# The middle phase of a long convolution, regrouped by pairs of frequencies

## The chip, the core and the metric

The kernel runs on one core of a Trainium2 chip. A core has a tensor engine (PE, which multiplies matrices into PSUM; its weight loads are listed as PEld), a vector engine (DVE), a scalar engine (ACT), GpSimd (POOL) and a sync engine (SP), which here only issues transfers. The engines run side by side and wait for each other by semaphores. DVE and ACT read PSUM, POOL does not. Transfers between HBM and SBUF are issued from SP's and ACT's queues and run on 16 DMA engines. The metric is the time of one execution on the device in microseconds (us); less is better.

## The reference

The input has 4 batches of 12800 positions with 128 channels. A small network with a decaying window makes a filter of the length of the sequence, one per channel. The product of `x` and `v` is convolved with it causally, by real Fourier transforms of twice the length; the result times `x` then passes a gated block.

```python
h_filt = (np.maximum(pos_emb @ w1, 0.0) @ w2) * window
u = x * v
Uf = np.fft.rfft(u, n=2 * S, axis=1)
Hf = np.fft.rfft(h_filt, n=2 * S, axis=0)
y = np.fft.irfft(Uf * Hf[None], n=2 * S, axis=1)[:, :S]
a = x * y
gate = sigmoid(sum(conv_w[k] * shifted(a, k) for k in range(5)))
out = (gate * (a @ w_val)) @ w_out
```

## The kernel before

The sequence is cut into two blocks (J = 2) of M = 6400 = N1 x N2 = 100 x 64 samples. Each block is evaluated at 6400 complex points, k = k1 + 100 k2, in two stages: a transform over 100 samples that yields k1, then one over 64 that yields k2. With U0, U1 the spectra of the two signal blocks and H0, H1' those of the filter (H1' is H1 - i H0), the inverse is applied to H0 U0 for the first block and to H0 U1 + H1' U0 for the second.

The kernel has three phases, one after the other.

Phase 1 makes the filter and the first stage of all spectra and stores the latter to HBM (`a_u`). Two of its matmuls, L200 and L201, give 64 columns each and write the two halves of PSUM's partitions. Phase 3 runs the inverse's second stage and the gated block. The change leaves both alone.

Phase 2 is a loop over the 100 values of k1. A step holds 128 partitions, the 64 real parts and the 64 imaginary parts of k2. It loads `a_u` (L351, two k1 a transfer) and the second stage's matrices (`wt`, eight k1 a transfer) from SP's queue. PE makes the filter's spectrum (`h_ps`, L360), which ACT copies to SBUF in four pieces (L364) so that one tile holds the real parts on both halves, the other the imaginary parts. PE makes the spectra of the two blocks (`z_ps`, L367), 4 batches x 128 channels each. A complex product needs real and imaginary part in the same partition; so ACT makes a copy `zsw` of `z_ps` with the halves exchanged and one of them negated (L299, L300). DVE multiplies `z_ps` by the filter's real parts (L311 for H0 U0 and H0 U1, L312 for H1' U0, into `v_t`), and POOL multiplies `zsw` by the imaginary parts (the same two lines, into `q_t`).

A step later DVE adds `q_t` to `v_t` (L316) and the second block's two terms (L317, 448 of 512 columns; POOL adds the other 64 two steps later, L320). Three steps later PE applies the inverse's first stage (`c_ps`, L326), ACT copies the result (L327) and issues its store to `c_y` (L328).

No planner reorders this: in the trace each engine runs phase 2's instructions in the order in which the loop writes them, and the framework puts the semaphores.

Of the kernel before, what the change touches and what calls it, by code (L numbers as in the profile page):

```python
# [9 lines left out]
F32 = mybir.dt.float32  # L10
F32R = mybir.dt.float32r
I32 = mybir.dt.int32
AF = mybir.ActivationFunctionType
ALU = mybir.AluOpType
# [3 lines left out]
# The causal convolution of length S = 2 * M is cut in two blocks of M = N1 * N2 samples,  # L18
# n = n1 * N2 + n2. A block's polynomial is evaluated at the M roots of z^M = i,
# k = k1 + N1 * k2, in two stages (over n1, then over n2 with the twiddles in the matrix).  # L20
# With z^M = i a product of two real blocks comes back as (low half) + i (high half), so
#   y0 = Re inv(H0 U0),   y1 = Re inv(H0 U1 + (H1 - i H0) U0)
# and no block is padded.
B, S, D, FO, KC = 4, 12800, 128, 64, 5
J, N1, N2 = 2, 100, 64
M = N1 * N2
KG = 8
# [6 lines left out]
def _tables():  # L34
# [10 lines left out]
    w = np.transpose(np.concatenate([f, g], 2), (1, 0, 2))  # L45
# [11 lines left out]
def _narrow(nc, pool, dst, src):  # L57
    """dst (float32) = src, whose 64-bit words are doubles, rounded to nearest."""
    p, n = dst.shape
# [12 lines left out]
    # the 29 bits below, in units of the value's own power of two  # L72
# [6 lines left out]
    # below float32's range: zero  # L79
# [7 lines left out]
def tile_longconv_gate(  # L87
# [24 lines left out]
    # spectra after the first stage: [k1][re|im][n2][block][...][d]  # L112
    a_u = dram.tile([N1, 2, N2, J, B, D], F32, name="a_u")
    # products after the inverse's first stage: [block][batch][k1][re|im, n2][d]
# [27 lines left out]
    def load():  # L142
        return ld.tile([128, 2048], F32, name="ld")
# [10 lines left out]
    # the filter's channels before w2, after the first stage: [re|im, n2][k1][block][channel]  # L154
# [4 lines left out]
    with tc.tile_pool(name="p1", bufs=1) as p1, tc.tile_pool(name="ps1", bufs=1, space=PSUM) as ps1:  # L159
# [4 lines left out]
        def filt():  # L164
# [25 lines left out]
            # block 1 holds H1 - i H0  # L190
# [14 lines left out]
            # the second stage, in place: [block, channel][k1][re|im, k2]  # L205
# [70 lines left out]
        # the filter's steps are spread over the signal's by their time on the tensor engine  # L276
# [16 lines left out]
    with tc.tile_pool(name="p2", bufs=1) as p2, tc.tile_pool(name="ps2", bufs=1, space=PSUM) as ps2:  # L293
        BD = B * D
        CUT = 64

        def tail(k1, g_l, z_ps, h_sb):
            zsw = p2.tile([128, J, BD], F32, name="zsw", bufs=2)
            nc.scalar.activation(zsw[0:N2], z_ps[N2:2 * N2], AF.Copy, scale=-1.0)  # L299
            nc.scalar.copy(out=zsw[N2:2 * N2], in_=z_ps[0:N2])  # L300

            def h_b(c, j, rep):
                a = h_sb[:, c, j]
                return a.unsqueeze(1).to_broadcast([128, rep, D])

            # [V0 | H0 U1 | H1' U0], then the last two added
            v_t = p2.tile([128, J + 1, BD], F32, name="v_t2", bufs=4)
            q_t = p2.tile([128, J + 1, BD], F32, name="q_t", bufs=3)
            fl = lambda t: t.rearrange("p j (b d) -> p (j b) d", d=D)
            for t, z, eng, c in ((q_t, zsw, nc.gpsimd, 1), (v_t, z_ps, nc.vector, 0)):  # L310
                eng.tensor_tensor(fl(t[:, 0:J]), fl(z), h_b(c, 0, J * B), op=ALU.mult)  # L311
                eng.tensor_tensor(fl(t[:, J:J + 1]), fl(z[:, 0:1]), h_b(c, 1, B), op=ALU.mult)  # L312
            return v_t, q_t

        def sums(v_t, q_t):
            nc.vector.tensor_tensor(v_t, v_t, q_t, op=ALU.add)  # L316
            nc.vector.tensor_tensor(v_t[:, 1, CUT:], v_t[:, 1, CUT:], v_t[:, 2, CUT:], op=ALU.add)  # L317

        def sums_rest(v_t, q_t):
            nc.gpsimd.tensor_tensor(v_t[:, 1, :CUT], v_t[:, 1, :CUT], v_t[:, 2, :CUT], op=ALU.add)  # L320

        def inverse(k1, g_l, v_t):
            c_sb = p2.tile([128, J, B, D], F32, name="c_sb", bufs=3)
            for j in range(J):
                c_ps = ps2.tile([128, BD], F32, name="c_ps", bufs=2)
                nc.tensor.matmul(out=c_ps, lhsT=g_l, rhs=v_t[:, j], start=True, stop=True)  # L326
                nc.scalar.copy(out=c_sb[:, j].rearrange("p b d -> p (b d)"), in_=c_ps)  # L327
            nc.scalar.dma_start(  # L328
                out=c_y[:, :, k1].rearrange("j b p d -> p (j b) d"),
                in_=c_sb.rearrange("p j b d -> p (j b) d"))  # L330

        SKEW = 3
        ready = []

        def advance(k1):
            for lag, do in ((1, sums), (2, sums_rest)):
                if 0 <= k1 - lag < N1:
                    do(*ready[k1 - lag][2:])
            if k1 >= SKEW:
                inverse(*ready[k1 - SKEW][:3])  # L340

        for k1 in range(N1):
            if k1 % KG == 0:
                n_k = min(KG, N1 - k1)
                wt = load().rearrange("p (k e) -> p k e", k=KG)
                nc.sync.dma_start(out=wt[:, 0:n_k], in_=t_w[:, k1:k1 + n_k])
            if k1 % 2 == 0:
                a2 = load().rearrange("p (k j e) -> p k j e", k=2, j=J)
                step = 1 if k1 == 0 else 2
                for i in range(0, 2, step):  # L350
                    nc.sync.dma_start(  # L351
                        out=a2[:, i:i + step].rearrange("p k j e -> p k (j e)"),
                        in_=a_u[k1 + i:k1 + i + step].rearrange("k c n j b d -> (c n) k (j b d)"))
            au = a2[:, k1 % 2]
            wk = wt[:, k1 % KG]
            f_l = wk[:, 0:2 * N2]
            g_l = wk[:, 2 * N2:4 * N2]

            h_ps = ps2.tile([128, J, D], F32, name="h_ps", bufs=2)
            nc.tensor.matmul(out=h_ps, lhsT=ag[:, k1].rearrange("p j e -> p (j e)"), rhs=w2bd, start=True, stop=True)  # L360
            h_sb = p2.tile([128, 2, J, D], F32, name="h_sb2", bufs=3)
            for c in range(2):
                for half in range(2):
                    nc.scalar.copy(out=h_sb[half * N2:(half + 1) * N2, c], in_=h_ps[c * N2:(c + 1) * N2])  # L364
            z_ps = ps2.tile([128, J, BD], F32, name="z_ps", bufs=2)
            for j in range(J):
                nc.tensor.matmul(out=z_ps[:, j], lhsT=f_l, rhs=au[:, j], start=True, stop=True)  # L367
            ready.append((k1, g_l) + tail(k1, g_l, z_ps, h_sb))
            advance(k1)
        for k1 in range(N1, N1 + SKEW):  # L370
            advance(k1)
# [5 lines left out]
    with tc.tile_pool(name="p3", bufs=1) as p3, tc.tile_pool(name="ps3", bufs=1, space=PSUM) as ps3:  # L377
# [5 lines left out]
        def conv_out(b, j, ext, rows=None):  # L383
            """y of one block, times x, transposed: ext[d, HALO + token]; with rows, a list
# [244 lines left out]
```

## Time and profile before

| what | value |
|---|---|
| median of 3 runs | 1739.79 us (1730.27 to 1749.66) |
| profiled execution, span of its instructions | 1744.1 us |
| mean granted clock of PE | 0.887 |
| busy in the span | PE 77%, DVE 81%, ACT 59%, POOL 67% |
| phase 2, first product of k1 = 0 to that of k1 = 98 | 478.1 to 1080.6 us |
| first load of `c_y` for phase 3 | issued at 1102.7 us |

A group's row gives line, engine, operation, output <- inputs, shapes and count, then the busy time in us and the mean of one in ns, then the idle time of the engine ahead of it and what ended most of it. A row of the timeline gives start and length in us, then the same names, and at the end the number of instructions merged into it. Busy time counts an instruction from its start, so time in which a started instruction is held up by another engine is counted as busy.

### The profile page before, as it was taken

How to read it: one execution, taken by the hardware profiler on the slowest of the kernel's cores; microseconds unless marked ns; L12 is line 12 of the kernel's file. 1: busy time of each engine (PE TensorE's matmuls, PEld its weight loads, DVE VectorE, ACT ScalarE, POOL GpSimd, SP SyncE). 2: the span in 40 equal slices, each digit the busy share in tenths (PEclk: the TensorE clock that was granted, in tenths of full speed). 3: DMA queues.
4: the chain of work that ended last, by engine and by line, in shares of the span. 5: the costliest groups of instructions: out<-in, count | busy, mean ns of one | idle time of the engine just before them, and what ended most of it. 6: DMA issues, size and time to landing. Idle time of an engine off the chain costs nothing.

```text
span 1744.1 us, 16766 instructions
## 1 busy us (share of the span) xinstructions
PE 1344.8 (77%) x5313; PEld 873.4 (50%) x5313; DVE 1418.7 (81%) x1204; ACT 1032.3 (59%) x1657; POOL 1168.2 (67%) x528
## 2 busy tenths in 40 slices
PE   4679988767677777677777676588888888889896
PEld 3567766544323333233333232356766676667675
DVE  5663337653399999999999999269999999999996
ACT  2235446552477777677777775255656565556765
POOL 2223333333299988878888888159978697788752
PEclk9798997885799989998999999687988998888899
DMA  6666666666656656555656553565555455555512
GB/s 227 243 243 241 246 236 234 241 235 253 220 203 198 212 181 205 179 177 181 203 178 211 173 185 99 170 216 168 183 191 158 159 183 161 172 177 166 177 61 91
DMA packets 224831, 332.97 MB, mean 191 GB/s; under 512 B 7832, under 2 KB 162500, under 8 KB 220108
## 3 DMA queue, kind: packets, MB, share of 16 engines
q1 hardware_dynamic: 99358, 226.12, 38.8%
q10 hardware_dynamic: 125386, 105.79, 18.3%
q8 instruction: 43, 0.70, 0.2%
q14 instruction: 44, 0.36, 0.1%
HBM read 200.80 MB, written 131.07 MB: 190 GB/s over the span
## 4 chain that ended last, share of the span: by engine, by line
DVE 43%; DMA 21%; issue 15%; PE 15%; ACT 3%; POOL 2%; SPq 1%; ACTq 0%; POOLq 0%; DVEq 0%
DVE gt L462 16%; DMA a_u<-st 13%; DVE v_t L316 9%; DVE v_t L317 5%; PE fp L264 4%; DMA ld<-c_y 4%; DVE v_t L311 3%; DVE v_t L312 3%; DMA ld<-in_x_dram 3%; DVE at L413 2%; PE o_ps L506 2%; DVE gd L495 2%; PE y_ps L412 2%; PE z_ps L367 1%; PE c_ps L326 1%
## 5 line engine op out<-in xcount | busy, mean ns | idle before, releaser
L447 POOL TENSOR_TENSOR lo<-ld,hi 100x1024 fp32r<-100x1024 f32 x117 | 373.0, 3209 | 116.9 <-ACT hi L444 115.2
L462 DVE SCALAR_TENSOR_TENSOR gt<-ext,cw,gt 128x1280 f32<-128x1280 f32 (+1 forms) x164 | 411.5, 2521 | 10.2 <-POOL gt L459 5.3
L238 POOL TENSOR_TENSOR u_lo<-u_t,u_hi 100x1024 fp32r<-100x1024 f32 x64 | 154.2, 2411 | 302.3 <-ACT u_hi L237 263.5
L367 PE MATMUL z_ps<-ld 128*128 128x512 f32 x400 | 215.7, 666 | 117.3 <-DVE v_t L312 97.7
L311 POOL TENSOR_TENSOR q_t<-zsw,h_sb 128x1024 f32<-128x1024 f32 x100 | 241.6, 2416 | 90.2 <-ACT zsw L300 90.2
L316 DVE TENSOR_TENSOR v_t<-v_t,q_t 128x1536 f32<-128x1536 f32 x100 | 277.6, 2806 | 1.2 <-POOL q_t L312 1.2
L326 PE MATMUL c_ps<-v_t,ld 128*128 128x512 f32 x400 | 208.0, 639 | 57.2 <-POOL v_t L320 29.1
L312 POOL TENSOR_TENSOR q_t<-zsw,h_sb 128x512 f32<-128x512 f32 x100 | 225.8, 2258 | 0.0
L364 ACT COPY h_sb<-h_ps 64x256 f32<-64x256 f32 x400 | 147.1, 368 | 103.0 <-DVE v_t L312 66.7
L264 PE MATMUL fp<-u_hi,fwd_hi 100*100 100x512 f32 x256 | 127.6, 499 | 90.3 <-ACT st L267 59.3
L269 DVE COPY st<-fp 100x512 f32<-100x512 f32 x128 | 84.6, 687 | 127.9 <-DMA a_u<-st 100.0
L367 PEld LDWEIGHTS z_ps<-ld 128*128 128x128 f32 x400 | 76.6, 206 | 205.8 <-issue 166.9
L506 PEld LDWEIGHTS o_ps<-wout,gd 128*128 128x128 f32 x700 | 167.9, 320 | 11.9 <-issue 2.5
L317 DVE TENSOR_TENSOR v_t<-v_t 128x448 f32<-128x448 f32 x100 | 172.6, 1757 | 0.1
L444 ACT CAST hi<-ld 100x1024 fp32r<-100x1024 f32 x128 | 128.0, 1048 | 71.1 <-DMA ld<-c_y 44.5
L326 PEld LDWEIGHTS c_ps<-v_t,ld 128*128 128x128 f32 x400 | 77.9, 205 | 179.2 <-issue 123.3
L506 PE MATMUL o_ps<-wout,gd 128*128 128x128 f32 x700 | 164.2, 384 | 0.7 <-DVE gd L495 0.7
L299 ACT ACTIVATE zsw<-z_ps 64x1024 f32<-64x1024 f32 x100 | 102.2, 1022 | 61.1 <-PE z_ps L367 56.9
L311 DVE TENSOR_TENSOR v_t<-z_ps,h_sb 128x1024 f32<-128x1024 f32 x100 | 121.1, 1211 | 18.5 <-ACT zsw L300 18.5
L267 ACT COPY st<-fp 100x512 f32<-100x512 f32 x128 | 69.7, 591 | 110.7 <-DMA a_u<-st 85.6
L237 ACT CAST u_hi<-u_t 100x1024 fp32r<-100x1024 f32 x64 | 68.0, 1064 | 107.1 <-PE fp L264 51.6
L236 DVE TENSOR_TENSOR u_t<-ld 100x1024 f32<-100x1024 f32 x64 | 82.5, 1290 | 57.0 <-POOL u_lo L238 49.9
(93 smaller groups left out, 2696.8 us busy)
## 6 DMA issues: line engine op xcount, KB each, us to landing
c_y<-c_sb ACTq DMA_DIRECT2D x100, 512.0 KB
ld<-c_y SPq DMA_DIRECT2D x64, 800.0 KB
ld<-a_u SPq DMA_DIRECT2D x49, 1024.0 KB
ld<-in_x_dram SPq DMA_DIRECT2D x66, 400.0 KB
ld<-in_v_dram SPq DMA_DIRECT2D x64, 400.0 KB
a_u<-st ACTq DMA_DIRECT2D x64, 400.0 KB
a_u<-st SPq DMA_DIRECT2D x64, 400.0 KB
ld<-in_x_dram SPq DMA_DIRECT2D x31, 800.0 KB
```

What stands on the lines that cost most here:

```text
L238: nc.gpsimd.tensor_tensor(lo, u_t, hi.bitcast(F32), op=ALU.subtract)
L264: nc.tensor.matmul(out=fp, lhsT=w[:, c], rhs=d[:, b:b + 2], start=(k == 0), stop=(k == 2))
L311: eng.tensor_tensor(fl(t[:, 0:J]), fl(z), h_b(c, 0, J * B), op=ALU.mult)
L312: eng.tensor_tensor(fl(t[:, J:J + 1]), fl(z[:, 0:1]), h_b(c, 1, B), op=ALU.mult)
L316: nc.vector.tensor_tensor(v_t, v_t, q_t, op=ALU.add)
L317: nc.vector.tensor_tensor(v_t[:, 1, CUT:], v_t[:, 1, CUT:], v_t[:, 2, CUT:], op=ALU.add)
L326: nc.tensor.matmul(out=c_ps, lhsT=g_l, rhs=v_t[:, j], start=True, stop=True)
L364: nc.scalar.copy(out=h_sb[half * N2:(half + 1) * N2, c], in_=h_ps[c * N2:(c + 1) * N2])
L367: nc.tensor.matmul(out=z_ps[:, j], lhsT=f_l, rhs=au[:, j], start=True, stop=True)
L447: eng.tensor_tensor(lo[:, :, hs], ct[:, :, hs], hi[:, :, hs].bitcast(F32), op=ALU.subtract)
L462: nc.vector.scalar_tensor_tensor(gt, sl(k), cw[:, k:k + 1], gt, op0=ALU.mult, op1=ALU.add)
L506: nc.tensor.matmul(out=o_ps[:, i], lhsT=gv[:, g0 + i], rhs=wout, start=True, stop=True)
```

## The change

Only phase 2 and the order of the table `w` change. The loop now goes over 50 pairs of k1. The two k1 of a pair lie on the two halves of the partitions, 64 k2 each, and real and imaginary parts lie in separate tiles. So a spectrum tile is made by two matmuls of 64 columns, one for each half, and an inverse tile by matmuls of 64 rows that add the real and the imaginary contribution in PSUM. ACT no longer exchanges halves; it copies the filter's spectrum as (real, imaginary) and as (-imaginary, real). All products are made by DVE from PSUM, the four of block 0 in two instructions 2048 wide, the two of block 1 in two 1024 wide. POOL only adds the two parts of the products, 2048 and 1024 wide. DVE adds the second block's two terms a pair later, and the inverse follows two pairs later. The PSUM banks `z_ps` are now four single ones, shared by filter and spectra; `c_ps` is two double ones.

The rest of the diff deletes comments. The functions `tail`, `sums`, `sums_rest`, `inverse` and `advance` and the loop over k1 that calls them go out; in their place comes:

```diff
 def _tables():
-    w = np.transpose(np.concatenate([f, g], 2), (1, 0, 2))
+    f = f.reshape(N1 // 2, 2, 2 * N2, 2 * N2).transpose(2, 0, 1, 3)
+    g = g.reshape(N1 // 2, 2, 2, N2, 2 * N2).transpose(1, 3, 0, 2, 4).reshape(2 * N2, N1 // 2, 2, 2 * N2)
+    w = np.concatenate([f, g], 2)
...
+        NP = N1 // 2
+        PG = KG // 2
+        half = [slice(h * N2, (h + 1) * N2) for h in range(2)]
+
+        def bank():
+            return ps2.tile([128, BD], F32, name="z_ps", bufs=4)
+
+        def filter_pair(p):
+            h_ps = bank().rearrange("p (c e) -> p c e", c=2)
+            for c in range(2):
+                for h in range(2):
+                    nc.tensor.matmul(
+                        out=h_ps[half[h], c], lhsT=ag[:, 2 * p + h].rearrange("p j e -> p (j e)")[:, half[c]],
+                        rhs=w2bd.rearrange("p j d -> p (j d)"), start=True, stop=True)
+            h_sb = p2.tile([128, 2, J, 2, D], F32, name="h_sb2", bufs=3)
+            src = h_ps.rearrange("p c (j d) -> p c j d", j=J)
+            nc.scalar.copy(out=h_sb[:, 0].rearrange("p j c d -> p c j d"), in_=src)
+            nc.scalar.activation(h_sb[:, 1, :, 0], src[:, 1], AF.Copy, scale=-1.0)
+            nc.scalar.copy(out=h_sb[:, 1, :, 1], in_=src[:, 0])
+            return h_sb
+
+        def spectrum(a2, wk, j, c):
+            z = bank()
+            for h in range(2):
+                nc.tensor.matmul(out=z[half[h]], lhsT=wk[:, h, half[c]], rhs=a2[:, h, j], start=True, stop=True)
+            return z
+
+        def times(out, z, h_sb, n):
+            nc.vector.tensor_tensor(
+                out, z.rearrange("p (b d) -> p b d", d=D).unsqueeze(1).to_broadcast([128, n, B, D]),
+                h_sb.unsqueeze(2).to_broadcast([128, n, B, D]), op=ALU.mult)
+
+        def products(p, a2, wk, h_sb):
+            va = p2.tile([128, 2 * J, B, D], F32, name="va", bufs=3)
+            vb = p2.tile([128, 2 * J, B, D], F32, name="vb", bufs=2)
+            vc = p2.tile([128, 2, B, D], F32, name="vc", bufs=3)
+            vd = p2.tile([128, 2, B, D], F32, name="vd", bufs=2)
+            h = h_sb.rearrange("p s j c d -> p s (j c) d")
+            times(va, spectrum(a2, wk, 0, 0), h[:, 0], 2 * J)
+            times(vb, spectrum(a2, wk, 0, 1), h[:, 1], 2 * J)
+            times(vc, spectrum(a2, wk, 1, 0), h[:, 0, 0:2], 2)
+            times(vd, spectrum(a2, wk, 1, 1), h[:, 1, 0:2], 2)
+            nc.gpsimd.tensor_tensor(va, va, vb, op=ALU.add)
+            nc.gpsimd.tensor_tensor(vc, vc, vd, op=ALU.add)
+            return va, vc
+
+        def sums(va, vc):
+            nc.vector.tensor_tensor(vc, vc, va[:, 2:4], op=ALU.add)
+
+        def inverse(p, wk, va, vc):
+            c_sb = p2.tile([128, 2, J, B, D], F32, name="c_sb", bufs=2)
+            for j, vt in enumerate((va, vc)):
+                c_ps = ps2.tile([128, 2, BD], F32, name="c_ps", bufs=2)
+                for c in range(2):
+                    for h in range(2):
+                        nc.tensor.matmul(
+                            out=c_ps[:, h], lhsT=wk[half[h], 2 + c], rhs=vt[half[h], c].rearrange("p b d -> p (b d)"),
+                            start=(c == 0), stop=(c == 1))
+                nc.scalar.copy(out=c_sb[:, :, j].rearrange("p h b d -> p h (b d)"), in_=c_ps)
+            for h in range(2):
+                nc.scalar.dma_start(
+                    out=c_y[:, :, 2 * p + h].rearrange("j b p d -> p (j b) d"),
+                    in_=c_sb[:, h].rearrange("p j b d -> p (j b) d"))
+
+        SKEW = 2
+        ready = []
+        for p in range(NP + SKEW):
+            if p < NP:
+                if p % PG == 0:
+                    n_p = min(PG, NP - p)
+                    wt = load().rearrange("p (k c e) -> p k c e", k=PG, c=4)
+                    nc.sync.dma_start(out=wt[:, 0:n_p], in_=t_w[:, p:p + n_p])
+                a2 = load().rearrange("p (k j e) -> p k j e", k=2, j=J)
+                step = 1 if p == 0 else 2
+                for i in range(0, 2, step):
+                    nc.sync.dma_start(
+                        out=a2[:, i:i + step].rearrange("p k j e -> p k (j e)"),
+                        in_=a_u[2 * p + i:2 * p + i + step].rearrange("k c n j b d -> (c n) k (j b d)"))
+                wk = wt[:, p % PG]
+                h_sb = filter_pair(p)
+                ready.append((p, wk) + products(p, a2, wk, h_sb))
+            if 1 <= p <= NP:
+                sums(*ready[p - 1][2:])
+            if p >= SKEW:
+                inverse(*ready[p - SKEW])
```

More of the change, by code (lines that the diff above doesn't have):

```diff
@@ L294, in tile_longconv_gate @@
         BD = B * D
[L295 to L330, printed above, removed]
@@ L332, in tile_longconv_gate @@
-        SKEW = 3
-        ready = []
[L335 to L347, printed above, removed]
+        NP = N1 // 2
@@ L348, in tile_longconv_gate @@
+        SKEW = 2
+        ready = []
+        for p in range(NP + SKEW):
[4 more added lines that the diff above has]
+                    nc.sync.dma_start(out=wt[:, 0:n_p], in_=t_w[:, p:p + n_p])
                 a2 = load().rearrange("p (k j e) -> p k j e", k=2, j=J)
-                step = 1 if k1 == 0 else 2
+                step = 1 if p == 0 else 2
                 for i in range(0, 2, step):
@@ L352, in tile_longconv_gate @@
                         out=a2[:, i:i + step].rearrange("p k j e -> p k (j e)"),
[L353 to L371, printed above, removed]
+                        in_=a_u[2 * p + i:2 * p + i + step].rearrange("k c n j b d -> (c n) k (j b d)"))
[6 more added lines that the diff above has]
+                inverse(*ready[p - SKEW])
     ag_pool.__exit__(None, None, None)
```

## The prediction

> **What bounds the kernel now.** I read the page first: its span, the slices and the costly groups.
>
> ```profile
> span 1744.1 us, 16766 instructions
> PE 1344.8 (77%) x5313; PEld 873.4 (50%) x5313; DVE 1418.7 (81%) x1204; ACT 1032.3 (59%) x1657; POOL 1168.2 (67%) x528
> DVE  5663337653399999999999999269999999999996
> ```
>
> The whole-span shares say little, because three stages follow each other. The middle stage is the unbroken run of nines on DVE. Asked for it alone, the windows view answers (columns: stretch, length, busy time and count on PE, PEld, DVE, ACT, POOL, then clock, DMA share, GB/s):
>
> ```profile
> 560.00:585.00 25.00, 17.53 (x43) 7.80 (x44) 25.00 (x19) 19.91 (x37) 25.00 (x15) 1.00 0.67 204
> 478.10:1080.60 602.50, 433.75 (x968) 185.11 (x968) 601.00 (x390) 443.92 (x776) 535.03 (x295) 0.94 0.58 186
> ```
>
> 478.1 and 1080.6 are the starts of DVE's first product for k1 = 0 and for k1 = 98, so 49 pairs took 602.5 us: 12.30 a pair. DVE is busy in 601.0 of it. Busy is not working, though; the groups and one period of the timeline show why.
>
> ```profile
> L316 DVE TENSOR_TENSOR v_t<-v_t,q_t 128x1536 f32<-128x1536 f32 x100 | 277.6, 2806 | 1.2 <-POOL q_t L312 1.2
> L317 DVE TENSOR_TENSOR v_t<-v_t 128x448 f32<-128x448 f32 x100 | 172.6, 1757 | 0.1
> L311 DVE TENSOR_TENSOR v_t<-z_ps,h_sb x100: 1209/1211/1226, 478.1 to 1088.8; 128x1024 f32<-128x1024 f32 x100
> 566.54 1.21 DVE L311 TENSOR_TENSOR v_t<-z_ps,h_sb 128x1024 f32<-128x1024 f32 x1
> 566.76 2.36 POOL L311 TENSOR_TENSOR q_t<-zsw,h_sb 128x1024 f32<-128x1024 f32 x1
> 567.67 0.68 DVE L312 TENSOR_TENSOR v_t<-z_ps,h_sb 128x512 f32<-128x512 f32 x1
> 568.27 2.46 DVE L316 TENSOR_TENSOR v_t<-v_t,q_t 128x1536 f32<-128x1536 f32 x1
> 569.08 2.78 POOL L312 TENSOR_TENSOR q_t<-zsw,h_sb 128x512 f32<-128x512 f32 x1
> 570.65 1.68 DVE L317 TENSOR_TENSOR v_t<-v_t 128x448 f32<-128x448 f32 x1
> 572.26 1.21 DVE L311 TENSOR_TENSOR v_t<-z_ps,h_sb 128x1024 f32<-128x1024 f32 x1
> ```
>
> L316 starts at 568.27 while POOL works until 566.76 + 2.36 = 569.12, and ends at 570.73: 1.61 after POOL's end. The POOL product behind it takes 2.78 instead of 1.28 (row below). So a DVE instruction with both inputs in SBUF and a POOL instruction exclude each other, and at POOL's end the waiting DVE instruction goes first. L311 and L312 on DVE read one input from PSUM; L311 took 1209 to 1226 ns in all 100 cases, POOL busy or not: they don't take part. These are the prices when nothing is in the way:
>
> ```profile
> 478.13 2.35 POOL L311 TENSOR_TENSOR q_t<-zsw,h_sb 128x1024 f32<-128x1024 f32 x1 [21.18 <-ACT zsw L300]
> 480.44 1.28 POOL L312 TENSOR_TENSOR q_t<-zsw,h_sb 128x512 f32<-128x512 f32 x1
> 1091.64 1.75 DVE L316 TENSOR_TENSOR v_t<-v_t,q_t 128x1536 f32<-128x1536 f32 x1
> 1093.42 0.62 DVE L317 TENSOR_TENSOR v_t<-v_t 128x448 f32<-128x448 f32 x1
> ```
>
> L316 averages 2.81 against 1.75 free, L317 1.76 against 0.62: 2.2 us of each k1 is DVE waiting for POOL. The middle stage is bounded by DVE and POOL taking turns.
>
> **The change, part by part. DVE.** Per pair it loses two L311, two L312, two L316 and two L317. It gets four products from PSUM, of 2048, 2048, 1024 and 1024 elements, and one sum of 1024 from SBUF. Start to start, 1024 elements cost 567.67 - 566.54 = 1.13 and 512 cost 0.60, so each further 512 cost 0.53 and 2048 cost 1.13 + 2 x 0.53 = 2.19 (no row has that width; at worst it is twice the 1024, 2.26). The products make 2 x 2.19 + 2 x 1.13 = 6.64. They exclude nobody, by L311's constancy. The sum, once it may run, takes 1.61 x 1024/1536 = 1.07.
>
> **POOL.** It loses all products (their cover, the ACT copies into zsw, goes too) and gets two additions, 2048 and 1024 wide. From 1.28 to 2.35 is 1.07 for 512 elements, so 2048 cost 2.35 + 2 x 1.07 = 4.49 (at worst 2 x 2.35 = 4.70).
>
> **The period.** Let va of pair p start at 0. vb ends at 2 x 2.19 + 0.08 = 4.46 (instructions start 0.08 before the one ahead ends: 566.54 + 1.21 against 567.67). POOL's wide addition starts about 0.1 later and ends at 9.05. DVE is through with vd at 6.64 and comes to the sum of pair p-1, whose inputs are long ready, but POOL is in its addition: DVE waits 2.4, goes first at 9.05 and ends at 10.12. POOL's narrow addition waits behind it, runs until 12.47, which is 2.4 into the next pair, and is done before the next wide one at 4.56. So a pair takes 10.1. The added wait sits in DVE's queue: behind it wait POOL's narrow addition and the next pair's products. Their spectra are in PSUM by then: four single banks go round among filter and spectra, and the next pair's first spectrum may be written as soon as vb is read, at 4.5, more than 5 us ahead of its use. With the worst widths it is 4.60 + 0.1 + 4.70 + 1.07 = 10.5.
>
> **PE.** Per pair the streamed columns double: 8 spectrum and 8 inverse matmuls of 512 columns for 4 and 4, and 4 filter matmuls of 256 for 2, each now on half of the array (64 columns, or 64 rows). Two passes make a matmul.
>
> ```profile
> 1079.50 1.88 PE L326 MATMUL c_ps<-v_t,ld 128*128 128x512 f32 x4
> 119.28 0.51 PE L174 MATMUL tp<-ident,ld 100*128 100x100 f32 x4
> 119.94 0.31 PE L200 MATMUL ap<-fwd,g_sb 100*64 100x100 f32 x1
> 119.95 0.31 PE L201 MATMUL ap<-fwd,g_sb 100*64 100x100 f32 x1
> 120.09 0.31 PE L200 MATMUL ap<-fwd,g_sb 100*64 100x100 f32 x1
> 120.10 0.31 PE L201 MATMUL ap<-fwd,g_sb 100*64 100x100 f32 x1
> 120.23 0.31 PE L200 MATMUL ap<-fwd,g_sb 100*64 100x100 f32 x1
> 119.98 0.25 PEld L200 LDWEIGHTS ap<-fwd,g_sb 100*64 100x64 f32 x1
> 120.12 0.25 PEld L200 LDWEIGHTS ap<-fwd,g_sb 100*64 100x64 f32 x1
> ```
>
> Four passes of 512 columns take 1.88 and four of 100 take 0.51, so a column costs (1.88 - 0.51)/(4 x 412) = 0.83 ns: 0.43 a pass of 512, 0.084 one of 100 (the rest is the last pass's tail). If the halves stream one after the other, a pair costs 16 x 0.43 + 16 x 0.43 + 8 x 0.215 = 15.5. If two halves stream at once it is half, 7.7. The filter's phase 1 already uses column halves (L200 and L201). Their passes start 0.01 apart where one alone streams for 0.084, so they overlap. But a couple of passes takes 0.147, not 0.084: a gain of only 2 x 0.084/0.147 = 1.14. Each weight load starts 0.11 ahead of its matmul, and that turnaround is longer than the stream of 100 columns; at 512 columns (0.43) I expect it hidden. I take 0.43 to 0.49 (0.43 plus the unhidden 0.063) for two halves: spectra and inverse 16 x 0.43 to 0.49 = 6.9 to 7.8, filter 4 x 0.215 to 0.28 = 0.9 to 1.1, together 7.8 to 8.9, under 10.1. The two ends are 7.7 and 15.5; I stay near the lower, the row of the same kind.
>
> The Trainium skill speaks against this in "TensorE: Matmul & The Clock Gate" (Part 3, The mechanism): a weight load overlaps a running matmul only if their row groups differ, and column halves share theirs. The trace disagrees: the load at 120.12 starts 0.03 after its half's matmul at 120.09, inside its stream. By that rule each couple would be 0.11 longer, 8 x 0.54 + 3.4 + 4 x 0.325 = 9.0, and the period would still be DVE's.
>
> No row has two row halves, as the inverse uses; they lie between 0.43 and 0.86 a couple, and I take the column halves' value. The Trainium skill, same page (Part 3, Measured speedup vs the span model), gives four row strips at once as 3.07 times one, by which row halves overlap too; no run here shows it.
>
> **ACT and DMA.**
>
> ```profile
> L364 ACT COPY h_sb<-h_ps 64x256 f32<-64x256 f32 x400 | 147.1, 368 | 103.0 <-DVE v_t L312 66.7 <-POOL q_t L312 23.3 <-DMA a_u<-st 9.1
> L327 ACT COPY c_sb<-c_ps 128x512 f32<-128x512 f32 x200 | 110.6, 588 | 18.0 <-PE c_ps L326 14.7
> L299 ACT ACTIVATE zsw<-z_ps 64x1024 f32<-64x1024 f32 x100 | 102.2, 1022 | 61.1 <-PE z_ps L367 56.9 <-POOL q_t L312 3.7
> 1099.39 0.37 ACTq L328 DMA_DIRECT2D c_y<-c_sb  x1
> ```
>
> ACT goes from 2 x (4 x 0.37 + 2 x 1.02 + 2 x 0.59 + 0.37) = 10.1 to 0.59 + 2 x 0.37 + 2 x 1.02 + 2 x 0.37 = 4.1 a pair: free. The loads and stores keep their bytes and number; the two stores of a pair are only issued together, behind both copies on ACT's queue, where nothing but the next pair's filter copies waits for them. Their 0.58 of the DMA engines over 12.30 becomes 0.58 x 12.30/10.1 = 0.71, a little over the 0.67 at which the stretch from 560 to 585 ran without a stall.
>
> **Sum.** 49 x (12.30 - 10.1) = 107.6. The ends I cost at nothing:
>
> ```profile
> 472.51 3.41 PE z_ps L367 x4
> 1080.62 1.21 DVE L311 TENSOR_TENSOR v_t<-z_ps,h_sb 128x1024 f32<-128x1024 f32 x1
> ```
>
> At the start, the first spectrum now needs two loads, but no longer the two ACT copies of 1.0 between 475.9 and 478.1: they trade within 2 us. At the end, from the last pair's start to the last store's issue it was 1099.8 - 1080.6 = 19.1; now it is 10.1 + 2.4 (narrow addition) + 1.1 (sum) + 1.7 to 3.4 (four couples, at 0.43 or at the cold 0.85 of the row above) + 1.0 + 0.7 = 17 to 18.7. Against the profiled span, 1744.1 - 107.6 = 1636.5. The median of the runs shown, 1739.8, lies 4.3 below that span, so 1632.
>
> **Rivals.** *The halves don't overlap enough (slower).* PE then sets the period. It decides from 10.1 on, an overlap under 15.5/10.1 = 1.5, and makes the kernel slower from 12.3 on, under 1.26. The 1.14 measured at 100 columns, taken as it stands, gives 13.6 a pair: 49 x 1.3 = 64 more, 1804; none at all gives 15.5, 157 more, 1897. For it: that 0.147. Against it: the starts 0.01 apart and a turnaround that doesn't grow with the columns. Chance 0.16.
>
> *Only the column halves overlap.* The inverse is 16 x 0.43 = 6.9, and PE 6.9 + 3.4 to 3.9 + 0.9 to 1.1 = 11.2 to 11.9; at 11.5 it is 49 x 0.8 = 39 less, 1701. Chance 0.09.
>
> *The transfers become the bound.* If 0.67 of the DMA engines is all that they give, a pair takes 0.58 x 12.30/0.67 = 10.65: 81 less, 1659. For it: no stretch here ran above 0.67. Against it: the page names no wait for these loads. Chance 0.07.
>
> *POOL's narrow addition goes first at 9.05.* The sum then waits for it too, 2.35 more, 12.45 a pair: 7 more, 1747, no change. The timeline speaks against it (L316 at 569.12 went ahead of POOL's L312). Chance 0.04.
>
> **Numbers.** The forecast case, 10.0 to 10.5 a pair, has 0.64: 1632, with the ends' 2 us and the runs' scatter (1730 to 1750) from 1610 to 1662. With the DMA case and the inverse's case up to 1701 and its scatter the range is 1610 to 1712; left out are 0.16 and 0.04. About 1% is what a measurement of this kernel can tell from no change. Faster: 0.64 + 0.07 + 0.09 = 0.80; same 0.04; slower 0.16.
>
> **What would show it.** In the profile after, DVE's products should be constant at about 2.28 and 1.21 us; its sum should show about 3.5 with its wait in it; POOL's wide addition 4.5 and its narrow one some 3.4 with its wait; the two halves' matmuls should start in couples 0.43 apart; DVE should stay at nine tenths, PE below. The forecast is wrong if DVE idles for z_ps, if couples of passes come 0.7 or more apart, if DMA ends waits of PE, or if the sum takes about 5.8.

## The result and the profile after

The changed kernel took 1672.34 us (median of four runs, 1669.55 to 1682.45) beside 1744.72 us for the kernel before, run beside it: a ratio of 0.9605, 95% interval 0.9542 to 0.9668. It is faster, inside the forecast's range, but the profiled span fell by 73.9 us (1744.1 to 1670.2) where the sum said 107.6. Ratios and intervals here and below, and e10's median, leave out one run of e10 that was slow at a lower granted clock (1768.5 us at 0.890; its other three 1725.4 to 1727.1 at 0.907 to 0.914).

The page of the changed kernel, its first lines and DVE's slices:

```profile
span 1670.2 us, 17347 instructions
PE 1353.8 (81%) x6313; PEld 831.4 (50%) x6313; DVE 1208.1 (72%) x1054; ACT 729.2 (44%) x1107; POOL 972.6 (58%) x328
DVE  5563336663457877787787786279989998998987
```

DVE's run of nines in the middle stage is gone; it stands at seven to eight tenths. The same from the windows view (columns as before), from the first `va` product to the last:

```profile
478.04:1022.76 544.72, 455.88 (x1940) 146.48 (x1938) 421.15 (x245) 152.89 (x243) 332.76 (x97) 0.96 0.64 206
```

544.72 / 49 = 11.12 us a pair, where 10.1 was forecast and 12.30 was before. Of a pair, DVE is busy for 421.15/49 = 8.59 and idle for 2.52. Who holds it up stands in the groups of the changed kernel between 478 and 1048 us:

```profile
L332 DVE TENSOR_TENSOR va<-z_ps,h_sb 128x2048 f32<-128x2048 f32 x50 | 114.0, 2281 | 18.6 <-PE z_ps L327 17.7 <-issue 0.8
L352 DVE TENSOR_TENSOR vc<-vc,va 128x1024 f32<-128x1024 f32 x50 | 101.6, 2032 | 125.6 <-POOL vc L348 125.6
L332 DVE TENSOR_TENSOR vc<-z_ps,h_sb 128x1024 f32<-128x1024 f32 x50 | 60.7, 1214 | 0.0
```

The products cost what was forecast (2.28 and 1.21 us). The sum L352 does not: ahead of it DVE stands idle for 125.6 us, always for POOL's narrow addition L348. A sum that stands where the loop writes it, behind vd of the pair after its own, would find that addition long done; so the sums must be issued earlier. The changed kernel's timeline of DVE shows its order, the last two rows what POOL does at the first of the three sums:

```profile
796.85 2.28 DVE L332 TENSOR_TENSOR va<-z_ps,h_sb 128x2048 f32<-128x2048 f32 x1
799.05 2.28 DVE L332 TENSOR_TENSOR vb<-z_ps,h_sb 128x2048 f32<-128x2048 f32 x1
801.72 5.51 DVE L352 TENSOR_TENSOR vc<-vc,va 128x1024 f32<-128x1024 f32 x1 [0.39 <-POOL vc L348]
807.16 1.21 DVE L332 TENSOR_TENSOR vc<-z_ps,h_sb 128x1024 f32<-128x1024 f32 x1
808.29 1.21 DVE L332 TENSOR_TENSOR vd<-z_ps,h_sb 128x1024 f32<-128x1024 f32 x1
809.42 2.27 DVE L332 TENSOR_TENSOR va<-z_ps,h_sb 128x2048 f32<-128x2048 f32 x1
811.98 1.23 DVE L352 TENSOR_TENSOR vc<-vc,va 128x1024 f32<-128x1024 f32 x1 [0.28 <-POOL vc L348]
813.12 2.28 DVE L332 TENSOR_TENSOR vb<-z_ps,h_sb 128x2048 f32<-128x2048 f32 x1
815.32 1.22 DVE L332 TENSOR_TENSOR vc<-z_ps,h_sb 128x1024 f32<-128x1024 f32 x1
816.45 1.22 DVE L332 TENSOR_TENSOR vd<-z_ps,h_sb 128x1024 f32<-128x1024 f32 x1
822.42 1.23 DVE L352 TENSOR_TENSOR vc<-vc,va 128x1024 f32<-128x1024 f32 x1 [4.75 <-POOL vc L348]
799.32 2.37 POOL L348 TENSOR_TENSOR vc<-vc,vd 128x1024 f32<-128x1024 f32 x1
801.63 4.52 POOL L347 TENSOR_TENSOR va<-va,vb 128x2048 f32<-128x2048 f32 x1
```

The loop writes va, vb, vc, vd, sum. Here the sum comes behind vb (801.72), behind va (811.98) and behind vd (822.42). At 801.72 it waits for the narrow addition and then through the whole wide one behind that: 5.51 us. At 822.42 it is the sum of the very pair whose vd has just run, and DVE idles 4.75 us for both additions. Counted over the 50 pairs, the sum stands behind vd of its own pair 20 times, behind va of the next pair 19 times and behind vb of the next pair 9 times; once it stands behind vc and once where the loop writes it. So the framework, when it builds the kernel, does order each engine's instructions anew; this part of it is called the planner below. The description of the kernel before says that no planner does; that is wrong, and the trace of before could have told it: only early in phase 2 (the quoted 566 to 573) do the four kinds of DVE's instructions come in the written order, and there too L317 is one step late. Later it looks like this, two sums of L316 and then two of L317 together:

```profile
1018.17 1.21 DVE L311 TENSOR_TENSOR v_t<-z_ps,h_sb 128x1024 f32<-128x1024 f32 x1
1019.31 0.68 DVE L312 TENSOR_TENSOR v_t<-z_ps,h_sb 128x512 f32<-128x512 f32 x1
1019.90 5.57 DVE L316 TENSOR_TENSOR v_t<-v_t,q_t 128x1536 f32<-128x1536 f32 x2
1025.39 1.21 DVE L311 TENSOR_TENSOR v_t<-z_ps,h_sb 128x1024 f32<-128x1024 f32 x1
1026.53 0.67 DVE L312 TENSOR_TENSOR v_t<-z_ps,h_sb 128x512 f32<-128x512 f32 x1
1027.12 4.42 DVE L317 TENSOR_TENSOR v_t<-v_t 128x448 f32<-128x448 f32 x2
```

The rest of the difference lies outside the period. From the last pair's first product to the first load of `c_y` it is 25.3 us (1022.76 to 1048.02) against 22.1 before, and phase 3, whose code is the same, takes 622.2 us against 641.4. The account: 57.8 from the periods, -3.1 from the end of phase 2, 19.2 from phase 3, together 73.9.

### The profile page after: what moved, and what is told of

The parts are those of the page before. It is cut to its first block, busy times and chain, and to the rows that moved or that the text cites. A ratio compares the mean times of both kernels' runs of the same rounds, so it can differ in the third digit from the quotient of the medians.

```text
span 1670.2 us, 17347 instructions
## 1 busy us (share of the span) xinstructions
PE 1353.8 (81%) x6313; PEld 831.4 (50%) x6313; DVE 1208.1 (72%) x1054; ACT 729.2 (44%) x1107; POOL 972.6 (58%) x328
## 5 line engine op out<-in xcount | busy, mean ns | idle before, releaser
L347 POOL TENSOR_TENSOR va<-va,vb 128x2048 f32<-128x2048 f32 x50 | 228.1, 4562 | 206.3 <-DVE vb L332 181.0
L363 ACT COPY c_sb<-c_ps 128x1024 f32<-128x1024 f32 x100 | 101.4, 1014 | 381.4 <-PE c_ps L360 370.2
L327 PE MATMUL z_ps<-ld 128*64 128x512 f32 x800 | 206.6, 623 | 24.1 <-DVE vb L332 11.3
L352 DVE TENSOR_TENSOR vc<-vc,va 128x1024 f32<-128x1024 f32 x50 | 101.6, 2032 | 125.6 <-POOL vc L348 125.6
L360 PE MATMUL c_ps<-vc,ld 64*128 64x512 f32 x400 | 125.3, 689 | 54.3 <-DVE vc L352 54.3
L348 POOL TENSOR_TENSOR vc<-vc,vd 128x1024 f32<-128x1024 f32 x50 | 118.6, 2372 | 29.7 <-DVE vd L332 29.7
L360 PE MATMUL c_ps<-va,ld 64*128 64x512 f32 x400 | 112.4, 626 | 19.2 <-POOL va L347 19.1
L332 DVE TENSOR_TENSOR va<-z_ps,h_sb 128x2048 f32<-128x2048 f32 x50 | 114.0, 2281 | 18.6 <-PE z_ps L327 17.7
L268 PE MATMUL fp<-u_hi,fwd_lo 100*100 100x512 f32 x256 | 117.6, 459 | 0.0
L430 PE MATMUL y_ps<-hi,inv_hi 100*100 100x512 f32 x256 | 100.6, 478 | 20.4 <-ACT hi L462 15.7
```

The costliest lines, as they stand in the source:

```text
L268: nc.tensor.matmul(out=fp, lhsT=w[:, c], rhs=d[:, b:b + 2], start=(k == 0), stop=(k == 2))
L327: nc.tensor.matmul(out=z[half[h]], lhsT=wk[:, h, half[c]], rhs=a2[:, h, j], start=True, stop=True)
L332: nc.vector.tensor_tensor(out, z.rearrange("p (b d) -> p b d", d=D).unsqueeze(1).to_broadcast([128, n, B, D]), h_sb.unsqueeze(2).to_broadc ...
L347: nc.gpsimd.tensor_tensor(va, va, vb, op=ALU.add)
L348: nc.gpsimd.tensor_tensor(vc, vc, vd, op=ALU.add)
L360: nc.tensor.matmul(out=c_ps[:, h], lhsT=wk[half[h], 2 + c], rhs=vt[half[h], c].rearrange("p b d -> p (b d)"), start=(c == 0), stop=(c == 1))
```

## The experiments

The theory after the result: the arithmetic of the forecast holds for the written order, and the planner's order is what was paid. To pin an instruction is to hold it, when the kernel is built, behind the one pinned before it on its engine. The rivals: the turns that DVE and POOL take cost more than reckoned; TensorE or the transfers hold the period. All kernels ran beside the kernel before (medians 1740.5 to 1745.6 us). "Period" is the mean from the first `va` product (before: every other step's first product) to the last, "end" from there to the first load of `c_y`.

| kernel | median us | ratio, 95% interval | period | end | phase 3 |
|---|---|---|---|---|---|
| changed kernel | 1672.3 | 0.9605 (0.9542 to 0.9668) | 11.12 | 25.3 | 622.2 |
| e1: DVE in written order | 1622.8 | 0.9329 (0.9262 to 0.9395) | 10.11 | 24.3 | 621.8 |
| e2: before, DVE in written order | 1699.8 | 0.9786 (0.9701 to 0.9871) | 11.38 | 22.0 | 635.1 |
| e3: sum on POOL | 1643.1 | 0.9448 (0.9379 to 0.9517) | 10.57 | 22.3 | 610.1 |
| e4: without additions | 1547.6 | one run | 8.75 | 14.8 | 625.7 |
| e5: e3 with PE and DVE in written order | 1579.1 | 0.9094 (0.9043 to 0.9146) | 9.06 | 33.4 | 617.5 |
| e6: sum of p-2 behind vb, PE and DVE in order | 1517.2 | 0.8728 (0.8686 to 0.8770) | 8.01 | 24.3 | 623.4 |
| e7: phase 3 in the order of before | 1685.9 | 0.9705 (0.9638 to 0.9772) | 11.12 | 24.7 | 632.8 |
| e8: e6, inverse issued row half by row half | 1522.9 | 0.8757 (0.8710 to 0.8803) | 8.11 | 23.7 | 618.9 |
| e9: changed kernel, PE and DVE in written order | 1628.2 | 0.9333 (0.9305 to 0.9362) | 10.10 | 23.9 | 623.7 |
| e10: e6, a spectrum between the row halves | 1725.4 | 0.9894 (0.9847 to 0.9941) | 12.16 | 28.1 | 621.2 |

### e1: the written order on VectorE

```diff
+        def pin(ins):
+            """ins is issued behind the one pinned before it, on the same engine"""
+            ins = getattr(ins, "ins", ins)
+            if last[0] is not None:
+                tc.add_manual_dep(
+                    ins, last[0].name,
+                    mybir.DependencyInfo(mybir.DependencyClass.NoSync, mybir.DependencyReason.DATA), reason="order")
+            last[0] = ins
...
-            nc.vector.tensor_tensor(vc, vc, va[:, 2:4], op=ALU.add)
+            pin(nc.vector.tensor_tensor(vc, vc, va[:, 2:4], op=ALU.add))
```

`times` is pinned in the same way. No semaphore is added; the instructions only keep their order.

> The changed kernel with DVE's order in phase 2 held to the order in which the loop writes it (products of pair p, then the sum of pair p-1); nothing else is different. Theory A (the forecast's period is right for the written order, and the miss is the place that the planner gave to the sum): 10.1 us a pair in place of 11.1, the sum lasting about 3.5 with its wait in every pair, DVE never idle for POOL's narrow addition, phase 2 shorter by 49 x 1.0 = 50 us, so about 1622 us if phase 3 stays as it is. Rival B (PE, with its banks and its halves, sets the period): the place of the sum matters little, 11 us a pair, about 1672. Rival C (the transfers): 10.65 a pair or more, with DMA share at 0.67 and PE waiting for ld.

Measured: 1622.76 us, and in the steady part 10.2 us a pair. DVE's and POOL's timeline of e1, one pair:

```profile
802.92 2.28 DVE L343 TENSOR_TENSOR va<-z_ps,h_sb 128x2048 f32<-128x2048 f32 x1
805.12 2.27 DVE L343 TENSOR_TENSOR vb<-z_ps,h_sb 128x2048 f32<-128x2048 f32 x1
807.32 1.21 DVE L343 TENSOR_TENSOR vc<-z_ps,h_sb 128x1024 f32<-128x1024 f32 x1
808.45 1.21 DVE L343 TENSOR_TENSOR vd<-z_ps,h_sb 128x1024 f32<-128x1024 f32 x1
809.58 3.58 DVE L363 TENSOR_TENSOR vc<-vc,va 128x1024 f32<-128x1024 f32 x1
807.54 4.54 POOL L358 TENSOR_TENSOR va<-va,vb 128x2048 f32<-128x2048 f32 x1 [2.33 <-DVE vb L343]
812.02 3.35 POOL L359 TENSOR_TENSOR vc<-vc,vd 128x1024 f32<-128x1024 f32 x1
```

This is the forecast's period line by line: the sum starts behind vd, waits for the wide addition until 812.08 and goes first, ending at 813.16; the narrow addition takes 3.35 with its wait inside. Moving one instruction back to its written place is worth 50 us. (PE's order also came out differently in e1 than in the changed kernel; e9, which holds PE's order too, takes as long as e1.)

### e2: the same for the kernel before

The diff pins L311, L312, L316 and L317 on DVE as e1 does.

> The kernel before with DVE's order in phase 2 held to the written one: products of k1, then both sums of k1-1. Theory A: it keeps the pace of the stretch from 560 to 585 us, 5.71 us a k1, for all of phase 2: 49 x (12.30 - 11.43) = 43 us less than before, about 1700. If the order of DVE has nothing to do with the slower pace after 620 us (rival: the clock or the transfers slow it down), it stays at 12.3 a pair and at the time of before.

Measured: 1699.78 us, 11.4 us a pair throughout; the sums take 2457 and 1569 ns with their waits instead of 2806 and 1757. So the kernel before paid 0.92 us a pair to the planner too, and in the written order the change takes 1699.8 to 1622.8, 77 us. What the forecast took away from 12.30 was a planned period, what it put in its place an unplanned one.

### e3: the sum on POOL

```diff
-            nc.vector.tensor_tensor(vc, vc, va[:, 2:4], op=ALU.add)
+            nc.gpsimd.tensor_tensor(vc, vc, va[:, 2:4], op=ALU.add)
```

> The changed kernel with the sum of the second block's two terms moved from DVE to POOL; no DVE instruction of phase 2 then has two SBUF inputs. Theory A: no exclusion is left, POOL works without a pause and sets the period, 4.5 + 2.35 + 2.35 = 9.2 us a pair, 94 us less than the 11.1 of the changed kernel, about 1578; POOL's additions show 4.5 and 2.35 without waits. Rival B (PE): 10 or more a pair with POOL idle. Rival C (transfers): DMA share stops at 0.67, 10.65 a pair, about 1650.

Measured: 1643.11 us. The waits of the additions go as expected, but the period settles at 10.8 us, not 9.2. PE's timeline of e3 tells why (a matmul is two entries, the x counts these):

```profile
799.78 1.12 PE L360 MATMUL c_ps<-vc,ld 64*128 64x512 f32 x2
800.84 1.08 PE L327 MATMUL z_ps<-ld 128*64 128x512 f32 x4
801.85 1.98 PE L360 MATMUL c_ps<-vc,ld 64*128 64x512 f32 x6
803.76 1.08 PE L327 MATMUL z_ps<-ld 128*64 128x512 f32 x4
804.77 1.98 PE L360 MATMUL c_ps<-va,ld 64*128 64x512 f32 x6
806.68 1.08 PE L327 MATMUL z_ps<-ld 128*64 128x512 f32 x4
807.69 1.12 PE L360 MATMUL c_ps<-va,ld 64*128 64x512 f32 x2
808.74 1.08 PE L314 MATMUL z_ps<-w2bd,ag 128*64 128x256 f32 x8
```

PE runs without a pause. The planner has put a spectrum inside each inverse tile: behind the third of its four matmuls for va, behind the first for vc. From start to start, the three take 1.91 us and the lone one 1.05: 2.96 for a tile, and 4 x 1.01 + 2 x 2.96 + 0.92 = 10.9 for a pair. That reading was put to the test in e5.

### e4: no additions

Leaves out POOL's two additions and DVE's sum; the inverse takes the unadded products, so part of the computation is missing.

```diff
-            nc.gpsimd.tensor_tensor(va, va, vb, op=ALU.add)
-            nc.gpsimd.tensor_tensor(vc, vc, vd, op=ALU.add)
...
-            nc.vector.tensor_tensor(vc, vc, va[:, 2:4], op=ALU.add)
+            pass
```

> The changed kernel without POOL's two additions and without DVE's sum, so that the inverse takes products that were not added; what is left of phase 2 is transfers, PE, ACT and DVE's four products. It shows the price of the rest alone. DVE's products are 6.64 a pair. PE by the rows of the changed kernel: a couple of passes every 0.43 within a spectrum or an inverse tile, some 0.2 more where one starts, so spectra 4 x 1.1, inverse 2 x 1.9, filter 1.1: about 9.3 if each starts on its own, 8.0 if they follow on. Theory A expects 8 to 9.3 a pair, bounded by PE. Rival B (PE cannot do a pair in less than the 11.1 of the changed kernel): 11. Rival C: DMA share stuck at 0.67, 10.65.

Measured: 1547.58 us, 8.75 us a pair, PE busy without a pause. The windows view of e4:

```profile
560.00:900.00 340.00, 340.00 (x1548) 105.94 (x1544) 260.69 (x155) 122.01 (x194) 0.00 (x0) 1.00 0.83 263
```

The DMA engines run at 0.83 and 263 GB/s, so 0.67 is no ceiling, and the rival of the transfers falls.

### e5: e3 in the written order

The pins of e1, and the same chain on PE over the matmuls of filter, spectra and inverse; the sum on POOL as in e3.

> Like e3 (the sum on GpSimd), and phase 2's matmuls and VectorE's products are issued in the written order, so the four matmuls of an inverse tile stand together again. Theory A (e3's 10.8 us a pair is TensorE's, because the matmuls of its inverse tiles were issued three and one and so met no partner: 2.96 us a tile in place of 1.92): the couples are back, two tiles give 2 us a pair back, and GpSimd's three additions are the bound, 4.53 + 2.36 + 2.36 = 9.25 us a pair. Phase 2 goes from e3's 10.57 us a pair in the mean to 9.3, 49 x 1.3 = 62 us less: about 1575 to 1585 us. Theory B (e3 is held by GpSimd's chain of three additions and the handing over between it and VectorE): the period stays between 10.5 and 10.8, 1640 us.

Measured: 1579.1 us, 64 less than e3, as the reading of e3 wanted: 9.3 us a pair in the steady part, which is POOL's three additions (4538, 2371 and 2355 ns). The mean in the table, 9.06, is lower because the products run ahead of POOL: its last wide addition starts at 937.1, 14.3 us behind the last `va` product, and the long end of 33.4 us holds the difference. In e5's timeline the eight entries of a tile stand together again, 1.91 from start to start:

```profile
705.76 1.99 PE L371 MATMUL c_ps<-vc,ld 64*128 64x512 f32 x8 [0.90 <-POOL vc L363]
707.67 1.08 PE L325 MATMUL z_ps<-w2bd,ag 128*64 128x256 f32 x8
```

### e6 and e9: where the sum stands

e9 is the changed kernel with PE and DVE pinned to the written order. e6 is e9 with the sum moved:

```diff
             times(vb, spectrum(a2, wk, 0, 1), h[:, 1], 2 * J)
+            between()
...
-        SKEW = 2
+        SKEW = 3
...
+                between = lambda: sums(*ready[p - 2][2:]) if p >= 2 else None
-            if 1 <= p <= NP:
-                sums(*ready[p - 1][2:])
+            elif p - 2 < NP:
+                sums(*ready[p - 2][2:])
```

`va` and `vc` get four buffers in place of three, `h_sb2` two.

> The sum stays on VectorE but is that of the pair before the last (p-2) and is issued right behind vb of pair p; phase 2's matmuls, products and sums are issued in the written order; va and vc have four buffers, h_sb2 two, and the inverse is that of p-3. Theory A (in e1 the sum waited 2.4 us for GpSimd's wide addition and pushed the narrow one behind it): the sum now finds its operands ready and lies beside no wait; VectorE has 2.28 + 2.28 + 1.07 + 1.21 + 1.21 = 8.05 us a pair, GpSimd's additions and the sum exclude each other for 4.53 + 2.36 + 1.07 = 7.96, TensorE needs the 8.75 to 8.8 that the run without additions shows. So 8.8 us a pair: 49 x (10.11 - 8.8) = 64 us less than e1's 1622.8, and up to 8 us more at the end for the pair more of skew: 1558 to 1568 us. Theory B (the additions and the sum, which take turns, hold the products up wherever the sum stands): the period stays at 9.5 or above, 1593 us or more.

> The changed kernel with phase 2's matmuls, products and sums all issued in the written order: between e1 (which holds VectorE's order alone, sum behind vd) and e6 (which also moves the sum). Theory A (e1's 10.1 to 10.2 us a pair is the wait of the sum for GpSimd's wide addition: 2.28 + 4.5 + 2.35 + 1.07 taken in turns by the shared port, TensorE not the bound): the period stays at 10.1 to 10.2 and the time at 1617 to 1627 us, so that all of e6's further 105 us come from where the sum stands. Theory B (e6 gains by TensorE's order, which also sets its 8.0 us a pair): the period falls to 9.2 or below, 1580 us or less.

Measured: e9 1628.2 us and 10.1 a pair, the same as e1, so PE's order adds nothing to DVE's there. e6 1517.18 us and 8.01 a pair, 41 us under the low end of what was expected: the 8.8 came from e4, whose PE order was also the planner's. DVE's and POOL's timeline of e6:

```profile
705.30 2.28 DVE L343 TENSOR_TENSOR vb<-z_ps,h_sb 128x2048 f32<-128x2048 f32 x1
707.50 1.22 DVE L364 TENSOR_TENSOR vc<-vc,va 128x1024 f32<-128x1024 f32 x1
708.63 1.22 DVE L343 TENSOR_TENSOR vc<-z_ps,h_sb 128x1024 f32<-128x1024 f32 x1
707.66 5.49 POOL L359 TENSOR_TENSOR va<-va,vb 128x2048 f32<-128x2048 f32 x1 [0.28 <-DVE vb L343]
```

The turns are still taken, but the other way round: the sum slips in at 707.50, just before vb's semaphore lets POOL start, and POOL's wide addition waits 1 us for it (5.49 in place of 4.53). That costs nothing, since POOL has time left. Before, DVE waited 2.4 us for POOL, and DVE had none. What the added buffers and the pair more of skew give without the new place of the sum was not tried. In the windows view of e6, PE and DVE are now both over nine tenths busy, and the transfers run at 0.86:

```profile
560.00:900.00 340.00, 324.18 (x1592) 125.68 (x1591) 310.93 (x198) 130.10 (x200) 308.60 (x80) 0.98 0.86 276
```

e6 beats both kernels of the study: 0.8728 of the time before.

### e7: phase 3

The code of phase 3 is the same before and after, but the planner's order of it is not: compared place by place, 300 of the 433 DVE instructions of phase 3 in the two traces are others. Save for single instructions, all kernels made from the changed one but e7 share one order there; the kernel before and e2 share the other. e7 is the changed kernel with phase 3 of PE, DVE, ACT and POOL chained, as in e1, in the order of before.

```diff
+        issued = nc.cur_bb.bb.instructions[p3_from:]
+        for eng, text in ORDER.items():
+            mine = [i for i in issued if str(i.engine).split(".")[-1] == eng]
...
+            for prev, ins in zip(seq, seq[1:]):
+                tc.add_manual_dep(
...
```

> The changed kernel with one thing more: phase 3's instructions on TensorE, VectorE, ScalarE and GpSimd are issued in the order that they have in the kernel before (the code of phase 3 is the same in both, the order is not). Theory A (phase 3's 19 us come from that order): phase 3 is 635 to 641 us, as in the two runs that have this order, in place of 622; the time is 13 to 19 us over the changed kernel's 1672.3: 1685 to 1691 us, ratio to the kernel before 0.966 to 0.970. Theory B (they come from the granted clock, or from what phase 2 leaves behind): phase 3 stays at 610 to 626 us and the time at 1672, ratio 0.960.

Measured: 1685.88 us. Phase 2 is as in the changed kernel (11.12 a pair), phase 3 is 632.8 us, just under the 635 to 641 expected. The three profiles with the old order have 632.8, 635.1 and 641.4, the nine with the new one in the table 610.1 to 625.7; the two ranges don't meet. So the order matters, though the intervals of e7's and the changed kernel's ratio still overlap. How much of the 19 us it makes is known only roughly: some 11 by e7 against the changed kernel (632.8 and 622.2), while profiles of one and the same order differ by up to 16 us. The mean granted clock of phase 3 is 0.88 in e2, e7 and the changed kernel, so it does not make these 11; in the kernel before it is 0.87, and whether that makes the other 8 is open. The groups of phase 3, of before, after and e7, show one place:

```profile
L462 DVE SCALAR_TENSOR_TENSOR gt<-ext,cw,gt 128x1280 f32<-128x1280 f32 (+1 forms) x164 | 411.5, 2521 | 10.2 <-POOL gt L459 5.3 <-ACT gt L455 4.5
```

```profile
L480 DVE SCALAR_TENSOR_TENSOR gt<-ext,cw,gt 128x1280 f32<-128x1280 f32 (+1 forms) x164 | 386.7, 2373 | 7.4 <-POOL gt L477 7.0
```

```profile
L563 DVE SCALAR_TENSOR_TENSOR gt<-ext,cw,gt 128x1280 f32<-128x1280 f32 (+1 forms) x164 | 407.4, 2496 | 11.3 <-POOL gt L560 6.5 <-ACT gt L556 4.5
```

The same 164 DVE instructions, with their inputs in SBUF, take 25 us more in the old order and 21 more in e7. That it is waiting for POOL's turn again is likely from phase 2, but was not tried by itself.

### e8 and e10: what two halves of the array are worth

e8 is e6 with the two loops around the inverse's matmul exchanged, so that both terms of row half 0 come ahead of both of row half 1:

```diff
-                for c in range(2):
-                    for h in range(2):
+                for h in range(2):
+                    for c in range(2):
```

e10 has this too, and lets a spectrum be issued between the two halves:

```diff
             times(va, spectrum(a2, wk, 0, 0), h[:, 0], 2 * J)
+            next(inv, None)
             times(vb, spectrum(a2, wk, 0, 1), h[:, 1], 2 * J)
+            next(inv, None)
...
+                    if h == 0 or j == 0:
+                        yield
```

> Like e6, but the four matmuls of an inverse tile are issued row half by row half (both terms of h = 0, then both of h = 1), not term by term. Theory A (two matmuls of different array halves run beside each other only where they are issued next to each other): of the four only the second and the third meet, a tile takes three places of about 0.98 us in place of two, so 2.0 us more a pair for its two tiles: 8.8 + 2.0 = 10.8 us a pair, TensorE the bound, 49 x 2.0 = 98 us over e6: about 1660 us. Theory B (the sequencer finds the partner by itself, whatever the order): the same time as e6. If no two of the four meet: 12.7 us a pair, about 1755 us.

> Like e6, but the two matmuls of row half 0 of an inverse tile and the two of row half 1 are issued with a spectrum (two matmuls that take all rows) between them, so that the two halves can never run beside each other. Theory A (a row half alone takes as long as both together: in e3's rows two matmuls of one half, or three of both, took 1.91 us, and a lone spectrum 1.01): TensorE has 0.92 + 4 x 1.01 + 4 x 1.91 = 12.6 us a pair in place of 8.0, 49 x 4.6 = 225 us over e6: about 1742 us, the kernel before again; this is the price of rival 1 for the inverse alone. Theory B (a half alone takes half the time, so that what counts is the work and not the overlap): 0.92 + 4 x 1.01 + 4 x 0.96 = 8.8 us a pair, about 1556 us.

Measured: e8 1522.94 us, its interval overlapping e6's; the 98 us of theory A did not come. e10 1725.4 us and 12.5 a pair in the steady part, near the 12.6 expected of halves that never meet. PE's timeline of e8, then of e10:

```profile
701.09 1.99 PE L372 MATMUL c_ps<-va,ld 64*128 64x512 f32 x8
702.91 1.99 PE L372 MATMUL c_ps<-vc,ld 64*128 64x512 f32 x8
```

```profile
702.69 1.08 PE L338 MATMUL z_ps<-ld 128*64 128x512 f32 x4
703.70 1.98 PE L376 MATMUL c_ps<-vc,ld 64*128 64x512 f32 x4
705.61 1.08 PE L338 MATMUL z_ps<-ld 128*64 128x512 f32 x4
```

In e8 four matmuls (eight entries) still take 1.82 us from start to start, two at a time, although only the second and the third are neighbours of different halves. In e10 two matmuls of one half (four entries) take 1.91 us, as long as four of both. So the halves overlap as long as no spectrum stands between them; the neighbourhood that e8's expectation supposed isn't needed. The Trainium skill, in "TensorE: Matmul & The Clock Gate" (Part 3, The mechanism), has matmuls start and end strictly in the order of the program; e8's time disagrees. In strict order the second matmul, of the first one's half, would run alone before the third could begin, and a tile would take three places of about 0.9 us and not two. The trace doesn't name the half of an entry, so that the third starts beside the first is inferred from these times. The starts of the single entries fit it: e8's `vc` tile runs in two rows, 702.92, 703.34, 703.77, 704.20 and 702.93, 703.45, 703.88, 704.31, each with its own delay.

## Why the prediction was partly right

The time was in the range, but the forecast case was not what happened: its 10.0 to 10.5 us a pair and 1610 to 1662 us stand against 11.12 and 1672. The range reached to 1712 only to hold the cases of the transfers and of the inverse, neither of which came; that the time fell into their part of it was luck. Of the signs named, the products' times came; the sum with its wait (about 3.5, measured 1.2 to 5.5), the narrow addition (some 3.4, measured 2.37) and DVE at nine tenths (seven to eight) did not.

**What bounds the kernel.** Right. DVE and POOL taking turns set the period before, and e1 shows the same after. The rule read from L316 (the waiting DVE instruction goes first) held to 0.1 us: sum 3.58 with its wait, narrow addition 3.35.

**Prices.** Products 2.28 and 1.21, start to start 2.20 and 1.13, against 2.19 and 1.13; wide addition 4.53 to 4.56 against 4.49. Nothing in the shortfall is a price.

**The period, the step that failed.** It is the sentence "DVE is through with vd at 6.64 and comes to the sum of pair p-1, whose inputs are long ready". The planner issued the sum earlier, behind vd of its own pair or behind va or vb of the next, so that it waits for additions that are not done: 2.51 us of idle DVE and 2.03 us of busy sum, 4.54 a pair where 3.5 was reckoned. The periods differ by 11.12 - 10.10 = 1.02, which is 49 x 1.02 = 50 us, and e1 gives just these back. The premise under it was the written order, read from the rows of 566 to 573 us, early in phase 2, and taken for the whole; the 12.30 set against it was not in written order either (e2: 11.38).

**PE.** Right: couples of halves 0.43 us apart. In e6 eight couples of a pair's spectra take 3.53 us, 0.44 each:

```profile
701.95 3.60 PE L338 MATMUL z_ps<-ld 128*64 128x512 f32 x16
705.48 1.99 PE L372 MATMUL c_ps<-va,ld 64*128 64x512 f32 x8
```

The Trainium skill, in "TensorE: Matmul & The Clock Gate" (Part 3, The mechanism), has weight loads overlap running matmuls only when the row groups differ. By the prediction's estimate from that rule a couple would take 0.54; the 0.44 measured disagrees, as the trace had suggested. A pair's least is 0.92 (filter) + 3.53 (spectra) + 1.82 + 1.81 (the two inverse tiles) = 8.08, inside the 7.8 to 8.9; e6 takes 8.01 a pair in the mean, so there PE sets the pace. What was missed is that this price holds for matmuls issued together, and that an isolated spectrum costs 1.01 in place of 0.88 and a split tile up to 2.96 (e3).

**The rivals.** Halves that don't overlap: not so, and e10 prices it, 12.5 a pair for the inverse alone, enough to spend all that the change gains. Only column halves overlapping: not so, a tile of row halves takes 1.82 us in e6, about half of the 8 x 0.43 = 3.4 that one after the other would need. The transfers: not so (0.83 in e4, 0.86 in e6). POOL's narrow addition first: not in e1. None of the four was what happened: an instruction issued elsewhere than written.

**The ends.** Reckoned at nothing; the end of phase 2 grew by 3.1 us. The last pair's sum of the pair before stood behind vb and took 5.50 us with its wait, so the last narrow addition started 12.7 us behind the last `va` product in place of 10.1 (1035.48 against 1022.76).

**Phase 3.** Reckoned as unchanged, and 19 us shorter; its code was unchanged, its order was not (e7 lays some 11 of the 19 to it). That this made up for part of the longer period was luck. Together: 1636.5 + 50 + 3 - 19 = 1670.5, the span measured. Without the shorter phase 3 the miss would have been 53 us.

## What to carry to other kernels

Before working out a period from the written order, follow one engine through several periods at both ends of the stage and see whether it keeps that order; if it doesn't, either pin it or cost the order that is there. An instruction that takes turns with another engine belongs where its operands are ready and the other engine is about to wait anyway: moving one 1 us sum from behind vd to behind vb, with a pair more of skew and the buffers for it, was worth 111 us here (e9 to e6). Where the code of a stage is unchanged, its order may still change with the code ahead of it.

## What the hardware showed

The two row halves of the array seem to work through their matmuls each for itself: issued half by half, four matmuls take 1.82 us, as they do issued term by term (e8, e6), and the two of one half alone take 1.91 (e10). A spectrum, which takes all rows and half the columns, ends the overlap when it stands between them: 12.5 us a pair in place of 8.0 (e10); which of the two properties does it was not tried. The DMA engines, which stood at 0.58 of their time in phase 2 of the kernel before, went to 0.86 and 276 GB/s with the same transfers closer together (e6).
